# Loading the first halves of k and v as float32 on SyncE's queue and casting them on the chip, with a new order of an attention and SoLU feed-forward kernel

## Chip, cores and metric

The kernel runs on one core of one Trainium2 chip. Its time is device microseconds of one execution; before the change it is 185.19 us, the median of 3 runs (184.95 to 185.66). Lower is better. The profile and the trace are of one execution of 185.46 us.

## What is computed

Linear attention for 8 batches, 8 heads, 576 positions of 64 (first a 64x64 product of k and v for each head, then q times it, then an RMS norm with gain `g_norm`), and behind it a feed-forward layer over 4608 tokens of 512 with 1024 hidden channels, a SoLU activation and a layer norm.

```python
def _attn_ref(q, k, v, g_norm) -> np.ndarray:
    kv = np.einsum('bhsd,bhse->bhde', k, v)
    out = np.einsum('bhsd,bhde->bhse', q, kv)
    rms = np.sqrt(np.mean(out * out, axis=-1, keepdims=True) + 1e-06)
    return (out / rms * g_norm).astype(np.float32)

def _moe_ref(x, w_in, w_out, g_ln) -> np.ndarray:
    h = x @ w_in
    h_max = np.max(h, axis=-1, keepdims=True)
    e = np.exp(h - h_max)
    sm = e / (np.sum(e, axis=-1, keepdims=True) + 1e-09)
    solu = h * sm
    mu = np.mean(solu, axis=-1, keepdims=True)
    var = np.mean((solu - mu) ** 2, axis=-1, keepdims=True)
    ln = (solu - mu) / np.sqrt(var + 1e-06) * g_ln
    return (ln @ w_out).astype(np.float32)
```

## The kernel before

The work is cut into nine token blocks of 512: blocks 0 to 7 are positions of one batch each, block 8 (`q_last`) holds the last positions of all batches. Every step is a named piece: `k.0.1` is the load of k for batch 0, half 1 of the heads (heads 4 to 7; half 0 is heads 0 to 3; from batch 2 on a load has all heads). A text, `ORDER`, lists all pieces by name, with the engine behind a colon where a piece may run on either of two; each engine runs its own pieces in that order. A second text, `ROOMS`, gives the buffer that each tile takes, and `WARM` the number of matmuls in each filler piece `warm.i`. A filler multiplies a tile of zeros (L296) and is read by nothing.

The pieces of one block, with their lines:

- `k`, `v`, `q` (L314), `w_in` (L333), `w_out` (L338): loads issued by POOL, on POOL's queue. k, v, q and w_in are float32 in memory and are cast to bfloat16 by the load. Eight semaphores serve these loads in turn, so the ninth waits until the first has landed. `g_rep` (L324): two loads on SP's queue that bring the 64 values of `g_norm` as a column, one value a partition; they wait for the first load of POOL (L143). `g_rows` (L254): g_ln as 8 rows of 128, on SP's queue.
- `ident` (L280): POOL makes two identity tiles. `turn_g` (L285): PE turns the rows of g_ln; `g_mean` (L287): DVE copies the result and spreads it over a tile for the mean of `w_out`.
- `kv_mm` (L364): PE multiplies k and v; `kv` (L232): three copies of the result a half, on DVE or ACT; `qT_mm` (L404) and `qT` (L232): PE turns q, DVE or ACT copies it out (blocks 4 to 8 are turned by SP's DMA, L412); `o_mm` (L423): q times kv.
- `sq` (L236, ACT), `s_mm` (L435, PE), `ex` (L449 in block 0, L443 later) with `ln` (L439) before it in blocks 1 to 8: the norm's factor; `x` (L455, DVE): o times `g_rep` times the factor. `table` (L460) is ACT's change of function table between block 0 and the rest.
- `h` (L492, PE): x times w_in, 8 column groups of 4 matmuls; in blocks 0 to 2 a group is two pieces, `h.c.f.0` with the first half of `w_in` and of x, `h.c.f.1` with the second. `exp` (L499, ACT), `u` (L503, DVE), `usq` (squares, L236 on ACT or L238 on POOL), `es` (sums of e, L511, POOL), `ua` and `usqa` (folds, L535, DVE), `sums` (L554, PE), `turn`, `stats`, `rstd`: the statistics of the layer norm.
- `w_mean` (L592) and `w_center` (L598): g_ln times `w_out`, less its mean over the channels; `out` (L611, PE): u times that; `ob` (L244 on DVE, L242 on ACT): times the norm's factor; `store` (L627; L623 for block 8).

What sets the order around the change is the head of `ORDER`:

```
v.0.1 k.0.1 q.0.1 ident q.0.0 v.0.0 k.0.0 q.1.0 k.1.0 v.1.0 warm.0 turn_g w_in.0 warm.1 kv_mm.0.1 warm.2 qT_mm.0.1
kv.0.1.1 kv.0.1.0:act qT.0.1:act warm.3 qT_mm.0.0 g_mean kv.0.1.2 o_mm.0.1 sq.0.1.0 warm.4 s_mm.0.1.0 w_in.1 v.1.1
```

Of the kernel before, what the change touches and what calls it, by code (L numbers as in the profile page):

```python
# [20 lines left out]
v.0.1 k.0.1 q.0.1 ident q.0.0 v.0.0 k.0.0 q.1.0 k.1.0 v.1.0 warm.0 turn_g w_in.0 warm.1 kv_mm.0.1 warm.2 qT_mm.0.1  # L21
kv.0.1.1 kv.0.1.0:act qT.0.1:act warm.3 qT_mm.0.0 g_mean kv.0.1.2 o_mm.0.1 sq.0.1.0 warm.4 s_mm.0.1.0 w_in.1 v.1.1
q.1.1 sq.0.1.1 s_mm.0.1.1 qT.0.0 ex.0.1.1 warm.5 kv_mm.0.0 kv.0.0.2:act kv.0.0.0:act kv.0.0.1:act warm.6 o_mm.0.0
ex.0.1.0 g_rep.0 k.1.1 g_rep.1 qT_mm.1.0 w_out.0 qT.1.0 w_out.1 x.0.1.1 x.0.1.0 sq.0.0.0 warm.7 s_mm.0.0.0 sq.0.0.1
warm.8 s_mm.0.0.1 ex.0.0.1 ex.0.0.0 table warm.9 kv_mm.1.0 q.2.0 x.0.0.1 kv.1.0.2 kv.1.0.1 kv.1.0.0 x.0.0.0 warm.10
o_mm.1.0 sq.1.0.0 warm.11 h.0.0.0 sq.1.0.1 v.2.0 k.2.0 s_mm.1.0.0 h.0.4.0 h.0.1.0 ln.1.0.0 h.0.2.0 s_mm.1.0.1 ex.1.0.0
ln.1.0.1 ex.1.0.1 x.1.0.0 h.0.3.0 h.0.0.1 h.0.3.1 h.0.1.1 h.0.4.1 exp.0.3 exp.0.4 q.3.0 u.0.3 h.0.5.0 exp.0.1 h.0.2.1
u.0.4 h.0.5.1 exp.0.2 x.1.0.1 qT_mm.1.1 h.0.7.0 qT.1.1 exp.0.5 exp.0.0 u.0.2 h.0.6.0 h.0.7.1 es.0.1 v.3.0 usq.0.4:act
h.0.6.1 u.0.0 u.0.5 u.0.1 exp.0.7 kv_mm.1.1 h.1.0.0 kv.1.1.2:act kv.1.1.1:act kv.1.1.0:act es.0.0 k.3.0 exp.0.6
o_mm.1.1 w_mean.0 u.0.7 u.0.6 ua.0.0 sq.1.1.1 w_mean.1 sq.1.1.0 s_mm.1.1.1 h.1.4.0 ln.1.1.1 s_mm.1.1.0 w_mean.2  # L30
w_mean.3 ln.1.1.0 ex.1.1.1 ua.0.1 ex.1.1.0 x.1.1.1 v.4.0 w_mean.4 w_mean.5 w_mean.6 w_mean.7 x.1.1.0 h.1.1.0
usq.0.2:act usq.0.3:act usq.0.0:act h.1.1.1 w_center.2 w_center.5 exp.1.1 h.1.0.1 qT_mm.2.0 h.1.2.0 usq.0.7 es.0.2
es.0.3 qT.2.0:act h.1.2.1 h.1.4.1 h.1.6.0 w_center.1 exp.1.2 h.1.6.1 exp.1.0 u.1.1 w_center.0 w_center.4 exp.1.6 u.1.2
usq.0.1 usq.0.6 h.1.7.0 h.1.7.1 exp.1.4 qT_mm.2.1 u.1.0 usq.0.5 exp.1.7 u.1.6 qT.2.1:act w_center.3 out.0.2.0 h.1.5.0
h.1.5.1 q.4.0 kv_mm.2.0 w_center.7 exp.1.5 q.5.0 h.1.3.0 w_center.6 es.1.2 h.1.3.1 kv.2.0.2 kv.2.0.0:act kv.2.1.0:act
kv.2.1.2:act kv.2.1.1:act kv.2.0.1:act out.0.1.0 usq.1.0:act o_mm.2.0 u.1.7 u.1.4 out.0.1.1 out.0.1.2 usq.1.1:act
usqa.0.0 sq.2.0.1 qT_mm.3.1 out.0.1.3 sq.2.0.0 u.1.5 exp.1.3 s_mm.2.0.1 out.0.2.1 s_mm.2.0.0 out.0.2.2 usqa.0.1
ln.2.0.1 u.1.3 usq.1.6:act usq.1.2 sums.0 qT.3.1 ln.2.0.0 out.0.2.3 usq.1.7 usq.1.4 ex.2.0.1 turn.0 o_mm.2.1 stats.0
qT_mm.3.0 sq.2.1.0 x.2.0.1 out.0.3.0 rstd.0 out.0.3.1 qT.3.0 es.1.0 ex.2.0.0 s_mm.2.1.0 out.0.3.2 ob.0.1 ln.2.1.0
out.0.3.3 x.2.0.0 kv_mm.3.0 sq.2.1.1 ob.0.2 ex.2.1.0 s_mm.2.1.1 kv.3.0.1 ln.2.1.1 kv.3.1.2 kv.3.0.2 kv.3.0.0 out.0.0.0  # L40
out.0.0.1 out.0.0.2 es.1.1 k.4.0 x.2.1.0 kv.3.1.1:act kv.3.1.0:act ex.2.1.1 o_mm.3.0 out.0.0.3 sq.3.0.0 x.2.1.1
h.2.0.0 usq.1.3 usq.1.5 sq.3.0.1 s_mm.3.0.0 ob.0.3 o_mm.3.1 ln.3.0.0 h.2.0.1 ob.0.0 store.0.3 sq.3.1.1 s_mm.3.0.1
out.1.1.0 ua.1.0 ln.3.0.1 store.0.1 exp.2.0 ex.3.0.0 usqa.1.0 sq.3.1.0 out.1.1.1 h.2.1.0 h.2.1.1 qT.4 x.3.0.0 es.1.3
h.2.3.0 h.2.3.1 ex.3.0.1 u.2.0 exp.2.1 h.2.5.0 x.3.0.1 exp.2.3 s_mm.3.1.1 es.2.0 h.2.5.1 u.2.1 ln.3.1.1 ex.3.1.1
h.2.7.0 h.2.7.1 u.2.3 ua.1.1 h.2.2.0 s_mm.3.1.0 exp.2.7 qT.5 h.2.2.1 x.3.1.1 usq.2.3 ln.3.1.0 h.2.4.0 u.2.7 h.2.4.1
exp.2.2 h.2.6.0 usqa.1.1 ex.3.1.0 store.0.2 h.2.6.1 u.2.2 exp.2.4 kv_mm.4.0 es.2.1 exp.2.5 es.2.2 usq.2.7 x.3.1.0
store.0.0 sums.1 u.2.4 h.3.4.1 kv.4.0.1:act turn.1 kv.4.1.0:act exp.2.6 kv.4.0.2 kv.4.1.2:act kv.4.1.1:act stats.1
h.3.5.1 kv.4.0.0:act exp.3.4 u.2.5 rstd.1 o_mm.4.1 u.2.6 h.3.2.1 exp.3.5 usq.2.1 ob.1.1 sq.4.1.1 h.3.6.1 u.3.5 exp.3.2
ua.2.0 s_mm.4.1.1 sq.4.1.0 out.1.3.0 exp.3.6 s_mm.4.1.0 u.3.4 ln.4.1.1 k.5.0 out.1.3.1 u.3.2 ln.4.1.0 o_mm.4.0 ob.1.3
ex.4.1.1 h.3.0.1 usq.2.2 v.5.0 sq.4.0.1 u.3.6 h.3.7.1 sq.4.0.0 x.4.1.1 q.6.0 ex.4.1.0 s_mm.4.0.1 s_mm.4.0.0 out.1.2.0  # L50
ln.4.0.1 x.4.1.0 q_last.0 ln.4.0.0 h.3.3.1 ex.4.0.1 h.3.1.1 es.3.2 es.2.3 ex.4.0.0 x.4.0.1 exp.3.3 out.1.2.1 x.4.0.0
usq.2.4:act exp.3.7 es.3.1 h.4.1.1 h.4.6.1 ob.1.2 usq.2.6:act u.3.3 exp.3.1 h.4.0.1 v.6.0 k.6.0 exp.4.6 u.3.1 usq.3.4
exp.3.0 kv_mm.5.0 u.4.6 exp.4.1 h.4.2.1 es.3.3 kv.5.0.1 kv.5.1.1 exp.4.0 kv.5.0.0:act kv.5.1.0 u.3.7 h.4.3.1 u.3.0
usq.2.5 exp.4.2 kv.5.0.2 h.4.7.1 kv.5.1.2:act exp.4.3 usq.2.0:act es.3.0 q.7.0 u.4.1 u.4.0 o_mm.5.1 out.1.0.0
out.1.0.1 u.4.2 sq.5.1.1 u.4.3 sq.5.1.0 usqa.2.0 exp.4.7 s_mm.5.1.1 s_mm.5.1.0 ln.5.1.1 out.2.3.0 ua.2.1 ln.5.1.0
h.4.5.1 ex.5.1.1 usqa.2.1 out.2.3.1 x.5.1.1 usq.3.0 exp.4.5 ob.1.0:act sums.2 usq.3.6:act o_mm.5.0 store.1.0 u.4.5
turn.2 stats.2 out.2.0.0 sq.5.0.1 sq.5.0.0 usq.3.5 u.4.7 out.2.0.1 store.1.1 ex.5.1.0 es.4.3 usq.3.2 s_mm.5.0.0
s_mm.5.0.1 qT.6 x.5.1.0 ln.5.0.0 out.2.1.0 ln.5.0.1 ua.3.0 out.2.1.1 ex.5.0.0 store.1.3 h.4.4.1 ex.5.0.1 x.5.0.0
rstd.2 x.5.0.1 kv_mm.6.0 exp.4.4 usq.4.6 out.2.2.0 kv.6.1.0:act kv.6.0.2 kv.6.0.1:act kv.6.1.2 usq.4.5:act
kv.6.1.1:act ob.2.0 es.4.0 usq.3.1 usq.3.7 h.5.7.1 ob.2.3 usq.3.3:act h.5.6.1 u.4.4 exp.5.7 store.2.3 h.5.3.1 u.5.7  # L60
kv.6.0.0:act usq.4.2:act ua.3.1 exp.5.6 o_mm.6.1 o_mm.6.0 exp.5.3 out.2.2.1 u.5.6 v.7.0 sq.6.0.1 u.5.3 es.4.2
out.3.3.0 ob.2.1 sq.6.0.0 s_mm.6.0.1 out.3.3.1 k.7.0 ob.2.2 sq.6.1.1 out.4.0.0 store.2.2 usqa.3.0 ln.6.0.1 sq.6.1.0
ex.6.0.1 s_mm.6.0.0 store.2.0 ln.6.0.0 out.4.0.1 s_mm.6.1.1 usqa.3.1 x.6.0.1 ex.6.0.0 es.4.1 h.5.2.1 store.1.2
ln.6.1.1 x.6.0.0 h.5.1.1 exp.5.2 qT.7 ex.6.1.1 s_mm.6.1.0 u.5.2 h.5.4.1 usq.4.7 usq.4.1 ln.6.1.0 x.6.1.1 sums.3
exp.5.4 out.3.0.0 turn.3 exp.5.1 es.5.3 stats.3 ex.6.1.0 u.5.4 rstd.3 es.5.1 x.6.1.0 out.3.1.0 h.5.0.1 u.5.1
# [616 lines left out]
```

## Time and profile before

| | |
|---|---|
| median of 3 runs | 185.19 us |
| the profiled execution | 185.46 us |
| its span in the profile | 183.2 us |
| PE busy | 173.1 us, 94% |
| ACT busy | 153.7 us, 84% |
| DVE busy | 142.0 us, 77% |
| POOL busy | 111.7 us, 61% |
| fillers on PE (`warm_ps`) | 44 recorded, 14.3 us |
| moved by DMA | 29.66 MB |

The span is measured from the program's first instruction to its last; the rest of an execution's time lies around it. PE is TensorE's matmuls, PEld its weight loads, DVE VectorE, ACT ScalarE, POOL GpSimd, SP SyncE. Matmuls are pipelined, so PE's busy time is more than the sum of its issue slots. A view lists the releaser behind an arrow: the event that ended the idle time before an instruction. "DMA to landing" is the time from a load's issue to its last byte. GB/s count the bytes as written, so a load that casts float32 to bfloat16 shows half of what it reads.

### The profile page before, as it was taken

How to read it: one execution, taken by the hardware profiler on the slowest of the kernel's cores; microseconds unless marked ns; L12 is line 12 of the kernel's file. 1: busy time of each engine (PE TensorE's matmuls, PEld its weight loads, DVE VectorE, ACT ScalarE, POOL GpSimd, SP SyncE). 2: the span in 40 equal slices, each digit the busy share in tenths (PEclk: the TensorE clock that was granted, in tenths of full speed). 3: DMA queues.
4: the chain of work that ended last, by engine and by line, in shares of the span. 5: the costliest groups of instructions: out<-in, count | busy, mean ns of one | idle time of the engine just before them, and what ended most of it. 6: DMA issues, size and time to landing. Idle time of an engine off the chain costs nothing.

```text
span 183.2 us, 4530 instructions
## 1 busy us (share of the span) xinstructions
PE 173.1 (94%) x1763; PEld 82.1 (45%) x1788; DVE 142.0 (77%) x263; ACT 153.7 (84%) x275; POOL 111.7 (61%) x120
## 2 busy tenths in 40 slices
...
GB/s 52 177 161 209 209 239 396 212 208 210 206 207 184 161 265 51 74 200 190 202 169 216 67 167 265 221 106 96 137 202 27 46 188 58 4 59 111 178 171 173
DMA packets 35030, 29.66 MB, mean 162 GB/s; under 512 B 16441, under 2 KB 28993, under 8 KB 35009
## 3 DMA queue, kind: packets, MB, share of 16 engines
...
q8 instruction: 14, 0.23, 0.5%
...
## 4 chain that ended last, share of the span: by engine, by line
PE 81%; ACT 9%; DVE 7%; issue 2%; ACTq 0%
PE out_ps L611 32%; PE h_ps L492 29%; PE warm_ps L296 6%; PE s_ps L435 4%; PE o_ps L423 3%; PE kv_ps L364 3%; DVE w_out_sb L598 3%; PE sum_ps L554 3%; ACT e_sb L499 3%; ACT osq_sb L236 2%; DVE x_sb L455 2%; ACT kvd L232 1%; DVE u_sb L503 1%; PE qt_ps L404 1%; ACT usq_sb L236 1%
## 5 line engine op out<-in xcount | busy, mean ns | idle before, releaser
L492 PE MATMUL h_ps<-x_sb,w_in_sb 128*128 128x512 bf16 x277 | 67.9, 379 | 1.5 <-DVE x_sb L455 1.0
L611 PE MATMUL out_ps<-w_out_sb,u_sb 128*128 128x512 bf16 x277 | 68.2, 379 | 0.9 <-issue 0.5
L511 POOL TENSOR_TENSOR es_sb<-e_sb 128x512 bf16<-128x512 f32 x36 | 45.6, 1277 | 24.3 <-DVE usq_sb L535 12.4
L503 DVE TENSOR_TENSOR u_sb<-h_ps,e_sb 128x512 bf16<-128x512 f32 x72 | 47.1, 683 | 4.7 <-ACT e_sb L499 4.3
L499 ACT ACTIVATE e_sb<-h_ps,zero_t 128x512 f32<-128x512 f32 x72 | 47.4, 691 | 3.2 <-PE h_ps L492 2.2
L238 POOL TENSOR_TENSOR usq_sb<-u_sb 128x512 bf16<-128x512 bf16 x34 | 34.9, 1041 | 13.0 <-DVE ua_sb L535 7.1
L492 PEld LDWEIGHTS <-w_in_sb 128*128 128x128 bf16 x288 | 27.2, 98 | 33.8 <-issue 3.2
L611 PEld LDWEIGHTS <-u_sb 128*128 128x128 bf16 x288 | 27.1, 98 | 32.2 <-issue 1.6
L455 DVE SCALAR_TENSOR_TENSOR x_sb<-o_ps,g_rep,rst_sb 128x512 bf16<-128x512 f32 x36 | 26.3, 746 | 9.5 <-ACT rst_sb L443 6.4
L236 ACT ACTIVATE usq_sb<-u_sb,zero_t 128x512 bf16<-128x512 bf16 x38 | 26.3, 723 | 0.2 <-DVE u_sb L503 0.2
L236 ACT ACTIVATE osq_sb<-o_ps,zero_t 128x512 bf16<-128x512 f32 x36 | 23.2, 692 | 1.7 <-PE o_ps L423 1.6
L443 ACT ACTIVATE rst_sb<-lss_sb,zero_t 128x512 f32<-128x512 f32 x32 | 22.7, 732 | 0.2
L439 ACT ACTIVATE lss_sb<-s_ps,eps_t 128x512 f32<-128x512 f32 x32 | 21.4, 695 | 0.8 <-PE s_ps L435 0.7
L244 DVE TENSOR_SCALAR ob_sb<-out_ps,rstd 128x512 f32<-128x512 f32 (+1 forms) x25 | 18.0, 735 | 5.1 <-PE out_ps L611 2.5
L535 DVE TENSOR_TENSOR usq_sb<-usq_sb 128x2048 bf16<-128x2048 bf16 (+1 forms) x18 | 17.1, 952 | 0.1
L296 PE MATMUL warm_ps<-zeros 128*128 128x512 bf16 x44 | 14.3, 452 | 1.6 <-DVE zeros L259 1.2
L232 ACT CAST kvd<-kv_ps 64x128 bf16<-64x128 f32 (+1 forms) x26 | 6.6, 263 | 10.2 <-DVE kvd L232 9.5
L232 DVE CAST kvd<-kv_ps 64x128 bf16<-64x128 f32 (+1 forms) x22 | 6.2, 287 | 9.5 <-PE kv_ps L364 8.8
L435 PE MATMUL s_ps<-osq_sb,head_mean 128*128 128x512 bf16 x36 | 13.0, 378 | 0.5 <-ACT osq_sb L236 0.2
L314 POOL DMA_DIRECT2D v_sb<-in_v_dram x10 | 7.7, 775 | 8.1 <-PE mean_ps L592 2.9
L242 ACT ACTIVATE ob_sb<-out_ps,rstd 128x512 f32<-128x512 f32 (+1 forms) x12 | 7.9, 668 | 5.6 <-PE out_ps L611 5.1
L535 DVE TENSOR_TENSOR ua_sb<-u_sb 128x2048 bf16<-128x2048 bf16 x9 | 10.9, 1217 | 0.0
...
## 6 DMA issues: line engine op xcount, KB each, us to landing
out_dram<-ob_sb SPq DMA_DIRECT2D x65, 128.0 KB, 2.4
v_sb<-in_v_dram POOLq DMA_DIRECT2D x6, 576.0 KB, 12.5
...
```

The lines of the kernel that those rows point to most:

```text
L236: nc.scalar.activation(out=dst, in_=src, func=AF.Square, bias=zero_t[:, :])
L238: on[engine].tensor_tensor(out=dst, in0=src, in1=src, op=MUL)
L296: nc.tensor.matmul(t[:, :], zeros[:, 0:128], zeros[:, :], start=True, stop=True)
L439: nc.scalar.activation(out=t[:, :], in_=T["s", i][:, :], func=AF.Ln, bias=eps_t[:, :])
L443: nc.scalar.activation(out=t.rearrange("p a b c -> p (a b c)"), in_=T["lss", i][:, :], func=AF.Exp, scale=-0.5, bias=zero_t[:, :])
L455: nc.vector.scalar_tensor_tensor(out=t[:, 2 * hf:2 * hf + 2, z], in0=T["o", c, hf, z][:, :, :, :], scalar=g_rep[:, :], in1=T["rst", (c, hf ...
L492: nc.tensor.matmul(bank(("h", c, f), [128, 512])[:, :], w_in_sb[:, dt, f * 128:(f + 1) * 128], T["x", c][:, dt].rearrange("p a b c -> p (a ...
L499: nc.scalar.activation(out=t[:, f % 2, :], in_=T["h", c, f][:, :], func=AF.Exp, bias=zero_t[:, :])
L503: nc.vector.tensor_tensor(out=t[:, f, :], in0=T["h", c, f][:, :], in1=T["e", c, f // 2][:, f % 2, :], op=MUL)
L511: on[engine].tensor_tensor(out=t[:, n, :], in0=e[:, 0, :], in1=e[:, 1, :], op=ADD)
L535: nc.vector.tensor_tensor(out=to[:, 0:n, :], in0=src[:, 0:n, :], in1=src[:, n:2 * n, :], op=ADD)
L611: nc.tensor.matmul(bank(("out", c, m), [128, d_model])[:, :], T["u", c][:, f, m * 128:(m + 1) * 128], w_out_sb[:, f, :], start=(f == 0), s ...
```

## The change

Four things are altered.

1. The first two loads, `k.0.1` and `v.0.1`, are split: a piece `wide.v` or `wide.k` loads the half as float32 on SP's queue, into a buffer of the `u` tiles, and the pieces `v.0.1` (DVE) and `k.0.1` (ACT) cast it to bfloat16.
2. `g_norm` is no longer spread by 64-row loads; it is loaded twice into one further row of `g_rows`, turned together with g_ln, and copied with it. `x` takes its column from there and so waits for `g_mean`. The loads of g stand behind the wide loads on SP's queue.
3. `WARM` goes from 12 fillers with 47 matmuls to 6 with 30.
4. `ORDER` and `ROOMS` are new throughout; some copies, squares and scalings change engine. The last two stores are both issued by ACT.

```diff
-14 11 3 3 3 1 2 1 1 3 3 2
+14 5 2 3 4 2
...
-    g_rep = big.tile([128, 1], FP32, name="g_rep")
...
-    nc.sync.dma_start(g_rows[:, :], moe_g_ln.rearrange("(n p) -> n p", p=128))
+    g_sb = big.tile([128, NF + 1], FP32, name="g_sb")
+    g_ln_sb, g_rep = g_sb[:, 0:NF], g_sb[:, NF:NF + 1]
+    g_rows = big.tile([NF + 1, 128], FP32, name="g_rows")
...
+    def load_g(_):
+        for half in range(2):
+            nc.sync.dma_start(g_rows[NF:NF + 1, 64 * half:64 * half + 64], g_norm[None, :])
+        nc.sync.dma_start(g_rows[0:NF, :], moe_g_ln.rearrange("(n p) -> n p", p=128))
...
-    add("turn_g", "pe", turn_g, ["ident"], [("g",)])
+    add("g_rows", "sp", load_g)
+    add("turn_g", "pe", turn_g, ["ident", "g_rows"], [("g",)])
...
+    def load_wide(name, src, hs):
+        t = kept_tile(("u", name), [128, NP // 2, 9 * D], FP32)
+        nc.sync.dma_start(t[:, :, :], rows_of(src, 0, hs, 9))
+
+    def narrow(engine, name, hs):
+        t = kept_tile((name, 0), [128, NP, 9, D], BF16)
+        copy(engine, t.rearrange("p n j d -> p n (j d)")[:, hs.start // 2:hs.stop // 2], T["u", name][:, :, :])
...
-    def load_g(half):
-        nc.sync.dma_start(g_rep[64 * half:64 * half + 64, :], g_norm[:, None])
...
+                if b == 0 and g == 1 and name != "q":
+                    add(("wide", name), "sp", lambda _, a=(name, src, hs): load_wide(*a), [], [("u", name)])
+                    add((name, b, g), "dve|act", lambda e, a=(name, hs): narrow(e, *a), [("wide", name)], [("u", name), (name, b)])
+                    continue
...
-                add(("x", i), "dve", lambda _, i=i: x_mul(*i), [("ex", i), ("g_rep", 0), ("g_rep", 1)], [("o", *i), ("rst", i), ("x", c)])
+                add(("x", i), "dve", lambda _, i=i: x_mul(*i), [("ex", i), "g_mean"], [("o", *i), ("rst", i), ("x", c)])
```

The head of the new `ORDER`:

```
wide.v v.0.1 wide.k k.0.1:act ident g_rows q.0.1 q.0.0 k.0.0 v.0.0 k.1.0 v.1.0 q.1.0 w_in.0 warm.0 qT_mm.0.1 w_in.1
qT.0.1:act kv_mm.0.1 turn_g kv.0.1.1 kv.0.1.2:act qT_mm.0.0 k.1.1 kv.0.1.0:act o_mm.0.1 qT.0.0 sq.0.1.1 sq.0.1.0 v.1.1
```

What this does to the queues is seen at three places. POOL's first work, before (the numbers tell buffers apart; `q_sb_150` comes twice, for half 1 and then half 0 of batch 0):

```order
L314 DMA v_sb_146<-in_v_dram 128x2x576
L314 DMA k_sb_148<-in_k_dram 128x2x576
L314 DMA q_sb_150<-in_q_dram 128x2x512
masks.py:197 MEMSET ident_77 128x128
masks.py:199 ISA
masks.py:199 AFFINE_SELECT ident_77<-ident_77 128x128 [waits Pool_49]
masks.py:197 MEMSET eye_78 8x8
masks.py:199 AFFINE_SELECT eye_78<-eye_78 8x8 [waits Pool_49]
L314 DMA q_sb_150<-in_q_dram 128x2x512
```

And now:

```order
masks.py:197 MEMSET ident_75 128x128
masks.py:199 ISA
masks.py:199 AFFINE_SELECT ident_75<-ident_75 128x128 [waits Pool_49]
masks.py:197 MEMSET eye_76 9x9
masks.py:199 AFFINE_SELECT eye_76<-eye_76 9x9 [waits Pool_49]
L320 DMA q_sb_163<-in_q_dram 128x2x512 x2
L320 DMA k_sb_150<-in_k_dram 128x2x576
L320 DMA v_sb_146<-in_v_dram 128x2x576
L320 DMA k_sb_168<-in_k_dram 128x2x576
```

The five instructions of `ident` stand ahead of the loads instead of behind the third, the two loads of k and v for half 1 are gone, and the loads begin with the two halves of q.

SP's first work, before (`g_rows` and `g_rep` are the loads of g_ln and g_norm, then come the stores of block 0 and the turns of q by DMA):

```order
L254 DMA g_rows<-in_moe_g_ln_dram 8x128
L324 DMA g_rep<-in_g_norm_dram 64x1 [waits DMASW0_49]
L324 DMA g_rep<-in_g_norm_dram 64x1
L627 DMA out_dram<-ob_sb 64x512 [waits DVE_49]
L627 DMA out_dram<-ob_sb 64x512 x3
```

And now:

```order
L326 DMA u_sb<-in_v_dram 128x2x576
L326 DMA u_sb<-in_k_dram 128x2x576
L279 DMA g_rows<-in_g_norm_dram 1x64 x2
L280 DMA g_rows<-in_moe_g_ln_dram 8x128
L639 DMA out_dram<-ob_sb 64x512 [waits DVE_49]
```

The two wide loads come first, without a wait; the loads of g follow them.

ACT's first work, before (`kvd` are the copies of the kv products, `osq` the squares of `sq`, `rst` the results of `ex`):

```order
L246 ACT_TABLE_LOAD
L232 CAST kvd_1_0_101<-kv_ps 128x128 [waits DVE_49]
L232 COPY qT_sb<-qt_ps 128x1024 [waits PE_49]
L236 ACTIVATE osq_sb<-o_ps,zero_t 128x512 [waits PE_49] x2
L449 ACTIVATE rst_sb<-s_ps,eps_t 128x512 [waits PE_49]
L232 CAST kvd_0_2_100<-kv_ps 64x128 [waits PE_49]
```

And now:

```order
L244 ACT_TABLE_LOAD
L230 CAST k_sb<-u_sb 128x1152 [waits DMAHW1_49]
L230 COPY qT_sb<-qt_ps 128x1024 [waits PE_49]
L230 CAST kvd_1_2_101<-kv_ps 64x128 [waits DVE_49]
L230 CAST kvd_1_0_99<-kv_ps 128x128
L234 ACTIVATE osq_sb<-o_ps,zero_t 128x512 [waits PE_49]
```

The cast of k stands ahead of everything else on ACT and waits for SP's second load (`DMAHW1`); the copy of q, the kv copies and the squares are queued behind it. On DVE the cast of v stands at the same place and waits for the first.

168 lines of the change are left out of this document (81 added, 87 removed).

## The prediction

> **What bounds the kernel now.** I read the stages first (busy time by stretch), then the chain of work that ended last, then the loads. The first rows are the profile page's span and its chain by engine; below them is the view by stretches (start:end in us, length, then busy us and instructions of PE, PE's weight loads, DVE, ACT and POOL, the granted clock, the DMA engines' busy share, GB/s).
>
> ```profile
> span 183.2 us, 4530 instructions
> PE 81%; ACT 9%; DVE 7%; issue 2%; ACTq 0%
> ```
> ```profile
> 0.00:7.00 7.00, 5.80 (x15) 2.02 (x15) 0.78 (x12) 1.28 (x1) 5.81 (x15) 1.00 0.65 94
> ...
> 16.00:22.20 6.20, 5.33 (x71) 2.40 (x72) 4.28 (x8) 5.17 (x9) 2.98 (x4) 1.00 1.15 211
> ...
> 26.00:38.00 12.00, 10.35 (x92) 5.48 (x93) 10.76 (x16) 11.81 (x23) 6.36 (x8) 1.00 1.24 294
> 38.00:50.00 12.00, 11.18 (x161) 5.93 (x162) 11.28 (x19) 11.03 (x21) 9.10 (x10) 1.00 1.22 208
> 50.00:66.00 16.00, 15.73 (x189) 7.40 (x181) 15.56 (x30) 15.88 (x30) 10.46 (x10) 1.00 1.16 195
> ...
> 140.00:179.40 39.40, 38.92 (x325) 18.09 (x328) 31.63 (x58) 30.52 (x54) 17.52 (x15) 1.00 0.42 102
> ```
>
> From 50 us on PE hardly rests (15.73 of 16, 38.92 of 39.4). What is saved before that moment is saved at the end; what is saved on another engine after it is not. Between 26 and 50 us ACT is the fullest (11.81 of 12, then 11.03) and DVE close behind. Before 22 us PE looks busy, but much of that is filler. The chain in order of time (start, us, what) says what was waited for:
>
> ```profile
> 1.20 5.80 PE warm_ps L296 x14
> ...
> 7.15 2.48 PE warm_ps L296 x11
> 9.63 0.69 PE kv_ps L364 x36
> ...
> 12.62 0.46 PE o_ps L423 x8
> ...
> 14.98 0.70 PE kv_ps L364 x36
> ...
> 15.71 0.26 ACT kvd L232
> ...
> 18.19 0.75 DVE x_sb L455
> ...
> 22.43 0.43 PE h_ps L492 x2
> ...
> 49.75 0.63 PE sum_ps L554 x32
> ...
> 179.43 0.48 ACT ob_sb L242
> ```
>
> The first 25 fillers end at 9.63, and then comes `kv_mm.0.1`. The second product, `kv_mm.0.0`, starts at 14.98, the first `h` at 22.43. So the kernel is a start of some 22 us, an ACT-bound stretch to about 50, and a PE-bound rest. Behind the last matmul lie 3.8 us to the span's end. The change acts on the start. What holds it up, with one group of instructions a line (start, us; in brackets idle time and releaser):
>
> ```profile
> 14.91 0.65 PEld L364 LDWEIGHTS <-k_sb 64*64 64x64 bf16 x36 [0.42 <-DMA k_sb<-in_k_dram]
> ...
> 20.33 1.28 ACT L460 ACT_TABLE_LOAD   x1
> ...
> 21.94 1.27 ACT L236 ACTIVATE osq_sb<-o_ps,zero_t 128x512 bf16<-128x512 f32 x2 [0.33 <-PE o_ps L423]
> ```
>
> `kv_mm.0.0` waits for a load, `k.0.0`. Issue and landing of single loads (issue time ahead of the dash, then us to landing):
>
> ```profile
> L314 POOL DMA_DIRECT2D v_sb<-in_v_dram x1: 890/890/890, 1.3 to 1.3; - x1
> DMA to landing us min/median/max: 4.3/4.3/4.3
> ```
> ```profile
> L314 POOL DMA_DIRECT2D k_sb<-in_k_dram x1: 733/733/733, 5.8 to 5.8; - x1
> DMA to landing us min/median/max: 8.6/8.6/8.6
> ```
> ```profile
> L333 POOL DMA_DIRECT2D w_in_sb<-in_moe_w_in_dram x2: 763/767/771, 8.7 to 9.4; - x2
> DMA to landing us min/median/max: 12.4/13.3/14.2
> ```
>
> `v.0.1` lands at 1.3 + 4.3 = 5.6, `k.0.0`, the sixth half load, at 5.8 + 8.6 = 14.4, the halves of `w_in` at 8.7 + 12.4 = 21.1 and 9.4 + 14.2 = 23.6. The loads run in a row: the start is bound by the bytes.
>
> **Term 1: the loads start earlier.** The same bytes are read before `w_in`, in nearly the same order. How fast, and when:
>
> ```profile
> 3.00:6.50 3.50, 3.50 (x10) 1.24 (x9) 0.00 (x0) 0.00 (x0) 3.35 (x8) 1.00 1.11 170
> ...
> 10.50:12.50 2.00, 2.00 (x21) 1.35 (x20) 1.29 (x4) 1.21 (x2) 0.73 (x1) 1.00 0.89 123
> ...
> 23.60:31.00 7.40, 7.35 (x73) 3.82 (x73) 4.93 (x8) 7.10 (x12) 3.75 (x5) 1.00 1.24 324
> ```
> ```profile
> 59.00:62.00 3.00, 3.00 (x16) 1.35 (x14) 3.00 (x4) 3.00 (x7) 0.81 (x1) 1.00 0.94 218
> ```
> ```profile
> out_dram<-ob_sb SPq DMA_DIRECT2D x65, 128.0 KB, 2.4
> ```
> ```profile
> 0.75 0.41 SPq L254 DMA_DIRECT2D g_rows<-in_moe_g_ln_dram  x1
> ```
> ```profile
> 3.56 0.23 POOL masks.py:197 MEMSET ident<- 128x128 bf16 x1
> ...
> 4.41 0.71 POOL L314 DMA_DIRECT2D q_sb<-in_q_dram  x1
> ```
>
> A half of k or v is 0.295 MB as bfloat16: 1.7 us at 170 GB/s. As float32 it is 0.59 MB: 1.8 us at the 324 GB/s that the uncast `w_out` reaches. The bytes cost the same; the clock of the first one moves. POOL issues its first load at 1.3; SP issues at 0.75. `v.0.1` needed 4.3 us, 1.7 of them bytes, so 2.6 of latency. On SP's queue a 128 KB store lands 2.4 us after issue (page, median), 0.4 of it bytes, so 2.0. Bounds: 0.5 us earlier (same latency) to 1.1 (store's latency); I take 0.9, nearer the row of SP's own queue. POOL's five `ident` instructions now stand ahead of its loads and delay `q.0.1` by 4.41 - 3.56 = 0.85, hidden under 3.6 us of SP's two loads. If these did not run, it would cost 0.85.
>
> **Term 2: the scattered g_norm goes.** Between 10.5 and 12.5 us the rate falls to 123 GB/s. That is when the two loads of `g_rep` are served, 64 rows of 4 bytes each:
>
> ```profile
> L324 SPq DMA_DIRECT2D g_rep<-in_g_norm_dram x2: 582/584/587, 5.6 to 6.2; - x2
> DMA to landing us min/median/max: 7.3/7.3/7.3
> ```
>
> Against 170 GB/s the two us lost 2.0 x 47 / 170 = 0.55 us of loading. Two rows of 256 bytes take their place; if the dip has another cause, the term is 0. I take 0.55.
>
> **Term 3: two queues at once.** SP's float32 and POOL's cast loads overlap for some 4 us. No row shows that. The nearest with both queues is 59:62 (stores beside loads), share 0.94 against 1.20 or so: up to 22% slower, 0.9 us; from below nothing, as one queue alone already fills the engines. I take 0, nearer the many stretches at 1.11 to 1.24, and keep 0.9 in the range. The Trainium skill ("DMA: Bandwidth & Descriptors", section "Queues, rings and completion order") says that each DMA engine goes round its queues packet by packet. By that rule the second SP load would share and land up to 1.8 later, near 8.6; the 7.3 us of `g_rep` are waiting of that kind, and the sum below holds with either value. So `k.0.0` and `v.0.0` are there at 14.4 - 0.9 - 0.55 = 13.0 (12.2 to 14.4), `w_in.0` at 19.6, `w_in.1` at 22.1.
>
> **Term 4: the two casts and the first half.**
>
> ```profile
> 11.55 1.01 ACT L232 COPY qT_sb<-qt_ps 128x1024 bf16<-128x1024 bf16 x1 [0.60 <-PE qt_ps L404]
> 10.88 0.69 DVE L289 TENSOR_SCALAR g_mean<-g_ln_sb 128x1024 fp32r<-128x1024 f32 x1
> ```
>
> 1152 elements cost, scaled by width, 1.1 us on ACT (k) and 0.8 on DVE (v). DVE and ACT are empty then. Wide k lands at 6.8 (alone) to 8.6 (shared); with the cast `kv_mm.0.1` starts at 8.0 to 9.8, against 9.6. Behind k's cast ACT holds the copy of `qT.0.1` (1.0), so `o_mm.0.1` at 9.6 to 11.4, squares (1.27), `s_mm`: PE is free for `kv_mm.0.0` at 11.6 to 13.4. That is beside the 13.0 of the load, so the first half costs 0 or, shared, 0.4. With g_norm turned with g, `x` now waits for `g_mean` on DVE, which stands at about 15, before the first `x`: 0.
>
> **Term 5: from kv_mm.0.0 to ACT's long run.** `kv_mm.0.0` at 13.15 to 13.85; then ACT in its new order: two kv copies (0.55), wait for `o_mm.0.0` (0.45), two squares (1.3), two `ex` (1.3), two kv copies (0.55), one `ex` (0.65), the table (1.3): 19.95. Then `sq.1.0`, which stood at 21.94: 2.0 us gained. The last `x` before `h` ends at 19.4, `w_in.0` lands at 19.6; `h` starts then. The fillers that go (47 to 30) stood in waits; they cost nothing now and give nothing.
>
> **Term 6: the rest of the order.** I counted the pieces on ACT between the table and the sums of token block 0: before 6 `sq`, 5 `ln`, 4 `ex`, 16 `exp`, 7 `usq`, 8 kv and 2 qT copies; now 8, 8, 6, 16, 3, 7 and 2. Seven pieces more, four `usq` and a kv copy fewer: at some 0.65 each (two squares take 1.27; kv 0.26) ACT's work grows by 1.75 us. But five pieces of PE that stood behind those sums now stand ahead of them: one `o_mm`, two `s_mm`, one `qT_mm` and two matmuls of `out`, together about 1.65 us (0.46 from the chain, 0.22 a matmul, 0.45). An end set by ACT up to the sums and PE after it moves by 1.75 - 1.65 = +0.1. Bounds by the rows: PE stands still for 24 - 10.35 - 11.18 = 2.5 us between 26 and 50; a better order could win 1, a worse one lose 2 more. The tail has the same four steps: 0.
>
> **Sum.** -2.0 + 0.1 = -1.9 on the profiled execution's 185.46 us (span 183.2 and 2.26 around it): 183.55. The median of the runs is 185.19, 0.27 lower: **183.3 us**.
>
> **Rivals.**
> 1. *SP's loads are starved by POOL's queue.* For it: `g_rep`'s 7.3 us for 256 bytes. Against it: SP's two loads are queued first. Price: wide k at about 10, `kv_mm.0.1` at 11.2, PE free for `kv_mm.0.0` at 14.6 instead of 14.9: gain 0.3 + 0.1, time 184.9.
> 2. *PE slows down (ends slower).* The chain shows 14 fillers at 0.41 us and the next 11 at 0.225: the array is slow until it has been busy some 5 us. With 16 fillers instead of 33 after the first 14 it could fall back between 7 and 19 us. Price: the start's products at double time (0.7 twice, and about 0.8 of o, qT and s) and 14 of `h` again at 0.19 more, 2.65: in all 4.9, less what waits hide (1.0): 183.3 + 3.9 = 187.2. It decides if the slow state returns before `h`; if only the start is hit and `h` not, the gain is just halved. Against it: the row of 44 to 46 us below, where PE is busy 1.31 of 2.00 and matmuls stay at full speed. In the Trainium skill ("TensorE: Matmul & The Clock Gate", section "Why this matters for your kernels") PE-idle gaps over about 3 us bring the half clock. By that rule the gap of 1 to 2 us behind the fillers does not.
> 3. *The new order stalls later.* Loads issued by POOL behind its squares (`v.3`) or ACT's seven extra pieces make PE wait. For it: ACT at 11.81 of 12. Price 1 to 3 us: 185.3.
> 4. *It doesn't do what it says:* loading is bound by bytes, not by the first one's clock, and the dip was not `g_rep`: 185.2.
>
> ```profile
> 44.00:46.00 2.00, 1.31 (x6) 0.59 (x6) 1.94 (x4) 1.10 (x6) 1.68 (x2) 1.00 1.21 213
> ```
>
> **Chances.** Forecast (182 to 184.2) 0.50, with a better order (below 182) 0.08; rival 1 0.09 and rival 4 0.05, both within 0.5%; rival 2 0.12 (0.10 of it slower); rival 3 0.16 (0.02 faster, 0.07 same, 0.07 slower). A measurement of this kernel can tell 0.5%, 0.9 us: faster means under 184.3, slower over 186.1. Faster 0.60, same 0.23, slower 0.17. The range 181.5 to 186.6 leaves out rival 2 and the best orders.
>
> **What would show it.** In the profile after: `k.0.0` landed near 13 and not 14.4; `kv_mm.0.1` between 8 and 10; the first `h` near 19.7; ACT's second table load ending near 20; the GB/s from 3 to 13 us without a dip to 123; fillers and early products at 0.22 us, not 0.41; the sums of block 0 near 48. I am wrong if `h` starts after 21, or if it starts early and PE stands still for more than 4 us between `h` and the sums.

## The result, and the profile after

The changed kernel takes 182.49 us, the median of 6 runs (182.00 to 183.04), against 185.29 us (184.95 to 185.86) for the kernel before on the same chip: a ratio of 0.9846, with a 95% interval of 0.9819 to 0.9873. It is faster by 2.8 us; 183.3 was forecast. The profiled execution took 182.66 us with a span of 180.5 us, against 185.46 and 183.2. One slow execution each of old_g_24 and fill_none, over 1.5% above the fastest of its kernel, is left out of the times below.

The page's span and its chain of work by engine, after the change:

```profile
span 180.5 us, 4509 instructions
...
PE 66%; DMA 21%; ACT 7%; DVE 3%; issue 1%; POOL 0%; POOLq 0%; ACTq 0%
```

DMA, which had no share of the chain before, now has 21%, PE 66% instead of 81%. Up to 40 us the chain is followed through loads. The same stretches as before the change (length, then PE, weight loads, DVE, ACT, POOL, the granted clock, DMA share, GB/s):

```profile
0.00:7.00 7.00, 5.36 (x14) 1.83 (x14) 1.67 (x13) 1.74 (x2) 6.31 (x16) 1.00 0.72 201
16.00:22.20 6.20, 5.69 (x71) 2.88 (x71) 2.86 (x5) 6.08 (x11) 1.88 (x4) 1.00 1.14 209
26.00:38.00 12.00, 11.16 (x102) 5.87 (x101) 11.63 (x18) 11.47 (x22) 10.07 (x10) 1.00 1.26 272
38.00:50.00 12.00, 11.36 (x246) 6.10 (x243) 11.47 (x21) 11.53 (x21) 8.03 (x10) 1.00 1.16 195
50.00:66.00 16.00, 16.00 (x194) 7.45 (x185) 15.48 (x32) 15.30 (x29) 11.36 (x11) 1.00 1.12 191
```

ACT is fuller from 16 to 22 us (6.08 of 6.2, before 5.17), and PE stands still for 1.5 us between 26 and 50 (24 - 11.16 - 11.36) where it stood still for 2.5. The steps of the start, in the timeline (start, length in us):

```profile
8.11 0.62 PE L416 MATMUL qt_ps<-ident,q_sb 128*128 128x128 bf16 x8 [1.56 <-DMA q_sb<-in_q_dram]
8.66 0.76 PE L376 MATMUL kv_ps<-v_sb,k_sb 64*64 64x64 bf16 x36
...
12.69 0.76 PE L376 MATMUL kv_ps<-v_sb,k_sb 64*64 64x64 bf16 x36
...
18.57 1.28 ACT L472 ACT_TABLE_LOAD   x1
...
19.78 1.03 PE L504 MATMUL h_ps<-x_sb,w_in_sb 128*128 128x512 bf16 x4
...
19.86 0.69 ACT L234 ACTIVATE osq_sb<-o_ps,zero_t 128x512 bf16<-128x512 f32 x1
...
40.60 0.78 PE L376 MATMUL kv_ps<-v_sb,k_sb 64*64 64x64 bf16 x72 [0.44 <-DMA k_sb<-in_k_dram]
...
48.74 0.30 PE L566 MATMUL sum_ps<-ua_sb,stat_sel 128*32 128x128 bf16 x8
```

`kv_mm.0.0` starts at 12.69 (before 14.98), `h` at 19.78 (22.43), `sq.1.0` at 19.86 (21.94), the sums of block 0 at 48.74 (49.75). The loads behind that (issue time ahead of the dash, then us to landing): wide k, `q.0.1`, `k.0.0`, `v.0.0` and the halves of `w_in`.

```profile
L326 SPq DMA_DIRECT2D u_sb<-in_k_dram x1: 454/454/454, 1.3 to 1.3; - x1
...
DMA to landing us min/median/max: 5.3/5.3/5.3
...
L320 POOL DMA_DIRECT2D q_sb<-in_q_dram x1: 882/882/882, 1.6 to 1.6; - x1
...
DMA to landing us min/median/max: 6.4/6.4/6.4
...
L320 POOL DMA_DIRECT2D k_sb<-in_k_dram x1: 716/716/716, 3.2 to 3.2; - x1
...
DMA to landing us min/median/max: 7.7/7.7/7.7
...
L320 POOL DMA_DIRECT2D v_sb<-in_v_dram x1: 721/721/721, 3.9 to 3.9; - x1
...
DMA to landing us min/median/max: 8.4/8.4/8.4
...
L342 POOL DMA_DIRECT2D w_in_sb<-in_moe_w_in_dram x2: 718/726/733, 6.8 to 8.4; - x2
...
DMA to landing us min/median/max: 12.5/13.0/13.5
```

They land at 6.6, 8.0, 10.9, 12.3, 19.3 and 21.9 us. Wide k is there at 6.6, yet PE's first product is the turn of q, and it waits for `q.0.1`. The dip is gone: between 10.5 and 12.5 us the engines move 207 GB/s instead of 123.

```profile
10.50:12.50 2.00, 1.81 (x15) 0.63 (x11) 0.42 (x1) 1.27 (x2) 0.74 (x2) 1.00 1.22 207
```

### The profile page after: what moved, and what is told of

Its sections match the earlier page's. It is cut to its first block, busy times and chain, and to the rows that moved or that the text cites. A ratio compares the mean times of both kernels' runs of the same rounds, so it can differ in the third digit from the quotient of the medians.

```text
span 180.5 us, 4509 instructions
## 1 busy us (share of the span) xinstructions
PE 171.3 (95%) x1771; PEld 80.5 (45%) x1771; DVE 143.4 (79%) x262; ACT 153.8 (85%) x276; POOL 112.1 (62%) x120
## 4 chain that ended last, share of the span: by engine, by line
PE 66%; DMA 21%; ACT 7%; DVE 3%; issue 1%; POOL 0%; POOLq 0%; ACTq 0%
PE out_ps L623 31%; PE h_ps L504 24%; DMA k_sb<-in_k_dram 10%; DMA w_in_sb<-in_moe_w_in_dram 7%; DMA q_sb<-in_q_dram 4%; PE s_ps L447 3%; PE sum_ps L566 2%; PE kv_ps L376 2%; ACT osq_sb L234 2%; PE o_ps L435 2%; DVE u_sb L515 1%; ACT e_sb L511 1%; ACT kvd L230 1%; ACT rst_sb L455 1%; DVE usq_sb L547 1%
## 5 line engine op out<-in xcount | busy, mean ns | idle before, releaser
L511 ACT ACTIVATE e_sb<-h_ps,zero_t 128x512 f32<-128x512 f32 x72 | 46.1, 696 | 2.2 <-PE h_ps L504 2.1
L236 POOL TENSOR_TENSOR usq_sb<-u_sb 128x512 bf16<-128x512 bf16 x36 | 37.0, 1042 | 13.8 <-DVE ua_sb L547 13.6
L467 DVE SCALAR_TENSOR_TENSOR x_sb<-o_ps,g_sb,rst_sb 128x512 bf16<-128x512 f32 x36 | 26.3, 746 | 9.2 <-ACT rst_sb L455 7.5
L234 ACT ACTIVATE usq_sb<-u_sb,zero_t 128x512 bf16<-128x512 bf16 x36 | 24.3, 720 | 1.7 <-DVE u_sb L515 1.7
L242 DVE TENSOR_SCALAR ob_sb<-out_ps,rstd 128x512 f32<-128x512 f32 (+1 forms) x27 | 19.3, 735 | 6.9 <-PE out_ps L623 3.4
L447 PE MATMUL s_ps<-osq_sb,head_mean 128*128 128x512 bf16 x36 | 13.5, 379 | 0.9 <-ACT osq_sb L234 0.6
L320 POOL DMA_DIRECT2D v_sb<-in_v_dram x9 | 6.9, 767 | 6.6 <-PE qt_ps L416 3.8
L298 PE MATMUL warm_ps<-zeros 128*128 128x512 bf16 x30 | 9.7, 468 | 1.2 <-DVE zeros L256 1.2
L230 DVE CAST kvd<-kv_ps 64x128 bf16<-64x128 f32 (+1 forms) x18 | 5.2, 288 | 6.8 <-PE kv_ps L376 6.1
L240 ACT ACTIVATE ob_sb<-out_ps,rstd 128x512 f32<-128x512 f32 (+1 forms) x10 | 6.6, 661 | 4.2 <-PE out_ps L623 4.2
L320 POOL DMA_DIRECT2D q_sb<-in_q_dram x10 | 7.6, 765 | 4.1 <-DVE ua_sb L547 2.1
```

The source lines that it names most:

```text
L234: nc.scalar.activation(out=dst, in_=src, func=AF.Square, bias=zero_t[:, :])
L236: on[engine].tensor_tensor(out=dst, in0=src, in1=src, op=MUL)
L242: nc.vector.tensor_scalar_mul(out=dst, in0=src, scalar1=by)
L467: nc.vector.scalar_tensor_tensor(out=t[:, 2 * hf:2 * hf + 2, z], in0=T["o", c, hf, z][:, :, :, :], scalar=g_rep, in1=T["rst", (c, hf, z)][ ...
L511: nc.scalar.activation(out=t[:, f % 2, :], in_=T["h", c, f][:, :], func=AF.Exp, bias=zero_t[:, :])
```

## The experiments

In each group the kernels ran on one chip beside the kernel before, and every ratio is against that. The changed kernel's is 0.9846. It ran on another chip than the groups below; differences to its 182.49 us are by medians, and the medians of the kernel before agree within 0.2 us (185.29 to 185.47).

**Undoing one load at a time: no_wide and old_g.** The first loads k and v of half 1 through POOL again:

```diff
-wide.v v.0.1 wide.k k.0.1:act ident g_rows q.0.1 q.0.0
+v.0.1 k.0.1 ident g_rows q.0.1 q.0.0
...
-                if b == 0 and g == 1 and name != "q":
+                if False:
```

> The changed kernel with one part undone: the first halves of k and v are loaded by POOL, cast on the way, ahead of ident and q.0.1; there is no float32 load and no cast on chip; order, g_norm and fillers as changed. Theory (the first load starts earlier on SP's queue and so all later ones): k.0.0 and v.0.0 land 0.9 to 1.3 us later than the 10.96 and 12.35 of the changed kernel, v.0.0 at 13.3 to 13.7, the first h at 20.7 to 21.1 instead of 19.78, and the run is 0.9 to 1.3 us longer than the changed one: about 183.5, 0.990 of the kernel before. Rival (the gain is g_norm's dip and the new order alone): h within 0.3 of 19.78, time 182.5, 0.985.

It took 184.15 us, 0.9933 (0.9907 to 0.9959): 1.7 us over the changed kernel, more than the loads were to cost. `v.0.0` landed at 13.3 and `w_in.0` at 20.6, `h` started at 21.07, all as the theory has it (1.0 to 1.3 us later). Some of the rest is in the clock. PE's timeline, from one of the faster executions (183.32 us):

```profile
8.27 0.88 PE L416 MATMUL qt_ps<-ident,q_sb 128*128 128x128 bf16 x8 [1.98 <-DMA q_sb<-in_q_dram]
9.07 1.17 PE L376 MATMUL kv_ps<-v_sb,k_sb 64*64 64x64 bf16 x36
```

and the stretch from 8.5 to 11.5 us, the third number from the right being the granted clock:

```profile
8.50:11.50 3.00, 2.90 (x52) 2.36 (x49) 0.29 (x1) 1.53 (x3) 2.37 (x4) 0.50 1.17 187
```

PE rested for 1.98 us, then had half its clock for 3 us: 36 small matmuls took 1.17 us instead of 0.76. The mean granted clock of every execution is on record, and such a spell takes it from 1.00 to about 0.99 (1.5 of 181 us): of the ten executions of no_wide one had 1.00 and was the fastest (183.16 us), eight had 0.986 to 0.991, and one, with 0.98, was the slowest (185.38). The rival (no gain from the wide loads) falls by `h`'s start. fill_few (below) ran beside no_wide and took 182.42 us, so the changed kernel's level holds on this chip too.

The second brings `g_norm` as 128 rows of 4 bytes again, now behind the two wide loads:

```diff
-            nc.sync.dma_start(g_rows[NF:NF + 1, 64 * half:64 * half + 64], g_norm[None, :])
+            nc.sync.dma_start(g_col[64 * half:64 * half + 64, :], g_norm[:, None])
...
-            out=t[:, 2 * hf:2 * hf + 2, z], in0=T["o", c, hf, z][:, :, :, :], scalar=g_rep,
+            out=t[:, 2 * hf:2 * hf + 2, z], in0=T["o", c, hf, z][:, :, :, :], scalar=g_col[:, :],
```

> The changed kernel with one part undone: g_norm comes again as 64 rows of 4 bytes, two loads on SP's queue behind the two float32 loads; all else as changed. Theory (each such load costs loading time, 0.55 us for the two): q.0.1 to w_in.1 land 0.4 to 0.6 us later, h at 20.2 to 20.4, time 182.9 to 183.1, 0.987 to 0.988. Rival (the dip was waiting of SP's queue behind POOL's and not a cost of the scattered rows): landings within 0.15 of the changed kernel's, time 182.5, 0.985.

185.02 us, 0.9979 (0.9960 to 0.9999): almost the whole gain is lost to 512 bytes, and both expectations were far too low. The loading rate between 5.5 and 9 us, old_g and then the changed kernel:

```profile
5.50:9.00 3.50, 1.72 (x5) 0.39 (x3) 0.54 (x1) 1.15 (x1) 2.12 (x3) 1.00 0.81 124
```
```profile
5.50:9.00 3.50, 1.94 (x33) 1.07 (x33) 0.46 (x1) 1.38 (x2) 2.69 (x4) 1.00 1.14 188
```

3.5 x (188 - 124) / 188 = 1.2 us of loading are lost, and `w_in.0` lands 1.3 us later, at 20.6. Here too the clock adds to it, behind a rest of 2.57 us:

```profile
9.79 0.62 PE L417 MATMUL qt_ps<-ident,q_sb 128*128 128x128 bf16 x8 [2.57 <-DMA q_sb<-in_q_dram]
10.34 1.17 PE L377 MATMUL kv_ps<-v_sb,k_sb 64*64 64x64 bf16 x36
```

**Taking the clock out of it: no_wide_18 and old_g_24.** More fillers ahead of the first product, to bridge the rest:

```diff
-14 5 2 3 4 2
+18 5 2 3 4 2     (no_wide_18)
+24 5 2 3 4 2     (old_g_24)
```

> The kernel no_wide with 18 fillers instead of 14 ahead of the first product, so that PE rests less than 1 us before q.0.1 has landed. Theory (no_wide lost time in two ways: its loads land 0.96 to 1.30 us later, and PE's granted clock falls to 0.50 for 3 us after a rest of 2 us): the clock stays at 1.00 from 8 to 12 us, kv_mm.0.1 takes 0.76 again and not 1.17, loads land as in no_wide (w_in.0 at 20.6), time 0.9 to 1.2 us over the changed kernel's: 183.4 to 183.7, 0.990 to 0.992. Rival (the later loads alone cost it, the clock is hidden in waits): 184.1, 0.9933 as no_wide.

183.93 us, 0.9933 (0.9910 to 0.9956). The four more fillers did not bridge the rest: all 18 ended at 6.5 us, since PE came to full speed sooner in the traced execution, so the rest was 2.12 us all the same and the half clock came back, only later, from about 10.7 to 14 us. But four of the six executions had a mean clock of 0.997 or more, so no such spell. Over both kernels, the five executions without a spell took 183.16 to 184.44 us (median 183.74), the ten with 0.986 to 0.991 took 183.32 to 184.91 (median 184.17). By that the later loads cost some 1.25 us and a spell about 0.4; the two groups overlap, so the second figure is uncertain.

> The kernel old_g (g_norm as 128 rows of 4 bytes) with 24 fillers instead of 14 ahead of the first product, so that PE rests less than 1 us before q.0.1 has landed at 9.75 us. Theory (two losses, as in no_wide: loads 1.2 to 1.6 us later, and PE's clock at 0.50 for 3 us): clock 1.00 throughout, w_in.0 at 20.6, h at 20.9 to 21.1, time 183.5 to 183.9, 0.990 to 0.993. Rival (the later loads alone): 185.0, 0.998.

183.69 us, 0.9926 (0.9903 to 0.9950), as the theory has it. In the trace PE rested for 0.69 us, the clock stayed at 1.00, and `kv_mm.0.1` took 0.76:

```profile
10.13 0.62 PE L417 MATMUL qt_ps<-ident,q_sb 128*128 128x128 bf16 x8 [0.69 <-DMA q_sb<-in_q_dram]
10.68 0.76 PE L377 MATMUL kv_ps<-v_sb,k_sb 64*64 64x64 bf16 x36
```

So of old_g's 2.5 us the scattered rows cost 1.2 by later loads (183.69 - 182.49), and 1.3 by the half clock that comes with their delay (185.02 - 183.69); by the ratios, which set off the chips, it is 1.5 and 1.0. The single executions bear the clock out. Four of old_g_24's five had a mean clock of 0.996 or more and took 183.53 to 183.79 us, the fifth, with 0.989, took 184.71. In old_g all twelve had less than 1: seven with 0.987 to 0.991 have a median of 184.83, five with 0.979 or 0.980, as of two spells, 185.50.

A long rest doesn't always bring the spell. pe_extra (below) has the start of the changed kernel, rested for 2.09 us in its traced execution, longer than no_wide, and kept its clock. PE's row and a stretch:

```profile
7.98 0.62 PE L416 MATMUL qt_ps<-ident,q_sb 128*128 128x128 bf16 x8 [2.09 <-DMA q_sb<-in_q_dram]
```
```profile
7.00:12.00 5.00, 3.68 (x66) 2.32 (x67) 0.98 (x2) 3.68 (x6) 2.39 (x4) 1.00 1.20 198
```

**Fillers: fill_few and fill_none.**

```diff
-14 5 2 3 4 2
+14 1 1 1 1 1     (fill_few)
+1 1 1 1 1 1      (fill_none)
```

> The changed kernel with 19 fillers (14 1 1 1 1 1) instead of 30 (14 5 2 3 4 2). Theory (fillers behind the first 14 stand in waits and neither cost nor help as long as PE stays at full speed): matmuls at 0.22 us through the start, time 182.5, 0.985. Rival (PE falls to its slow state with fewer fillers): products and h at 0.41 us a matmul for a while after 10 us, h about 0.7 to 1.5 later, up to 3.9 in all: 183.2 to 186.4, 0.989 to 1.006.

182.42 us, 0.9842 (0.9819 to 0.9865): no difference. PE now rested for 1.37 us in the middle of the start and stayed fast:

```profile
12.14 0.59 PE L447 MATMUL s_ps<-osq_sb,head_mean 128*128 128x512 bf16 x2 [1.37 <-ACT osq_sb L234]
```

> The changed kernel with 6 fillers (1 at each of the six places) instead of 30, so that PE hardly works before 8 us. Theory: PE is in its slow state from 8 us until it has been busy some 4 us; the first products, o, qT and s take double time (0.7 twice, some 0.8 and some more), h starts 1.0 to 2.5 us later and its first dozen matmuls may still be slow: 183.5 to 186.4, 0.990 to 1.006. Rival (the slow state is hidden in the waits for loads): h within 0.5 of 19.78, time 182.5 to 183.0, 0.985 to 0.988.

184.25 us, 0.9939 (0.9909 to 0.9969): 1.8 us over the changed kernel, in the theory's window; `h` came 2.8 us later in the traced execution (185.49 us), more than it allowed. Without the first 14 fillers PE is slow from its first product to the first `h`, and its first four matmuls still take 1.16 us together instead of 1.03:

```profile
8.83 1.17 PE L376 MATMUL kv_ps<-v_sb,k_sb 64*64 64x64 bf16 x36
...
22.59 1.16 PE L504 MATMUL h_ps<-x_sb,w_in_sb 128*128 128x512 bf16 x4 [0.34 <-DVE x_sb L467]
```

The granted clock reads 1.00 through all of this. The half speed that PE starts at isn't seen in that column here, only in the matmuls' own lengths; the one that comes back after a rest (no_wide, old_g) is seen in both.

**Parts of the change on the old order: b_rows and b_wide_rows.** The first is the kernel before with only the rows of `g_norm`; the second has the wide loads and fewer fillers as well. Everything else runs in the order of before.

```diff
-v.0.1 k.0.1 q.0.1 ident q.0.0
+v.0.1 k.0.1 q.0.1 ident g_rows q.0.0                        (b_rows)
+wide.v v.0.1 wide.k k.0.1:act q.0.1 ident g_rows q.0.0      (b_wide_rows)
...
```

> The kernel before with one part of the change: g_norm as two rows of 256 bytes, issued on SP's queue at the start and turned with g; no float32 loads, order and fillers as before. Theory (each of the 128 rows of 4 bytes takes engine time wherever it is served): no dip at 10.5 to 12.5 us, k.0.0 lands 0.5 to 1.5 us before 14.45, w_in.0 as much before 21.10, first h at 21.0 to 21.9 instead of 22.4, time 184.0 to 184.9, 0.992 to 0.997. Rival (it cost so much only in old_g, where q.0.1 stood behind it): landings within 0.2, time 185.4, 1.000.

184.54 us, 0.9950 (0.9931 to 0.9969). `k.0.0` landed at 13.5 (before 14.4), `w_in.0` at 20.6 (21.1), and `h` started at 21.67. The rate from 9.5 to 12.5 us, before and in b_rows, and what the engines were doing in that time before (queue, packets, MB, share of 16 engines; q1 is SP's queue):

```profile
9.50:12.50 3.00, 2.84 (x58) 2.13 (x58) 1.43 (x4) 1.21 (x2) 1.37 (x2) 1.00 1.00 145
```
```profile
9.50:12.50 3.00, 2.84 (x45) 1.93 (x40) 1.89 (x5) 1.30 (x3) 1.47 (x3) 1.00 1.20 199
```
```profile
q0 software_dynamic: 403, 0.43, 95.1%
q1 hardware_dynamic: 151, 0.00, 5.3%
```

SP's 151 packets took 5.3% of the engines by their own time, but a quarter of the rate. Their price doesn't stand in their own duration; it is read from what the other queue lost. The theory holds, the rival falls.

> The kernel before with the float32 loads, the rows of g_norm and fewer fillers (14 3 3 3 1 1 1 1 1 1 2 2), but the order of before for all else. Theory (most of the gain is the earlier start of h, and before's order gets at least half of it): k.0.0 at about 12.3, h at 20.3 to 21.3 since before's order has more on ACT ahead of it, time 183.4 to 184.4, 0.989 to 0.995; what is left to 182.5 is the new order's. Rival (the parts need the new order to pay): h at 21.5 or later, time 184.8 or more, 0.997 and over.

184.29 us, 0.9935 (0.9913 to 0.9958). Time, `h` and `k.0.0` fall into the theory's windows, but the old order gets 0.65% of the 1.54%, not quite the half. The interval overlaps that of b_rows: on the old order the wide loads bring nothing that can be told (0.25 us by the medians), though `w_in.0` landed 1.65 us earlier than there, at 19.0. PE's timeline, from the slowest of the six executions (185.08 us):

```profile
13.62 0.76 PE L380 MATMUL kv_ps<-v_sb,k_sb 64*64 64x64 bf16 x36
...
18.35 0.75 PE L380 MATMUL kv_ps<-v_sb,k_sb 64*64 64x64 bf16 x36 [0.28 <-DVE x_sb L471]
...
20.98 0.59 PE L508 MATMUL h_ps<-x_sb,w_in_sb 128*128 128x512 bf16 x2
...
83.00 0.77 PE L380 MATMUL kv_ps<-v_sb,k_sb 64*64 64x64 bf16 x72 [0.78 <-DVE u_sb L519]
```

`k.0.0` was there at 12.0, but `kv_mm.0.0` started at 13.62, and `h` at 20.98, 2 us after its load. Here the chain of pieces is late, not the loads: it lets 0.69 us through to `h` (21.67 in b_rows). As much is still there at the sums of block 0 (48.45 against 49.14) and of block 1 (66.37, 67.06). Behind them it is lost, in this execution by the wait of 0.78 us at 83 us, which b_rows doesn't have, and by 0.6 us from the last sums to the last `ob` (7.05 us, in b_rows 6.46). b_wide_rows also has other buffers (`ROOMS`) than b_rows; whether these bring the waits, and whether the faster executions have them too, no run here shows.

The new order, with its fillers and its choice of engines, is worth 1.8 us on top (184.29 - 182.49, the intervals apart). `h` starts 1.2 us earlier with it (19.78). The sums of block 0 come as late (48.74), but with the new order some 1.65 us of PE's work that stood behind them is done by then. The new order without the other parts was not run.

**What binds between `h` and the sums: act_extra, pe_extra, load_extra.**

```diff
-        nc.scalar.activation(out=t[:, f % 2, :], in_=T["h", c, f][:, :], ...)
+        for _ in range(2 if c == 0 and f in (1, 5) else 1):
+            nc.scalar.activation(out=t[:, f % 2, :], in_=T["h", c, f][:, :], ...)
```

> The changed kernel with exp.0.1 and exp.0.5 executed twice each, so that ACT has 1.3 us more to do between 24 and 31 us and nothing else is touched. Theory A (the stretch from h to the sums of block 0 is ACT's, as the prediction has it): the sums and the end 1.0 to 1.3 us later, 183.5 to 183.8, 0.990 to 0.992. Theory P (PE's, from the first h on): 0 to 0.3 us, 182.5 to 182.8. Theory L (the loads' up to k.2 at 40.56 us): 0 to 0.4 us, 182.5 to 182.9, 0.985 to 0.987.

183.67 us, 0.9899 (0.9871 to 0.9928): 1.2 us later for 1.3 us of work, as theory A has it. The sums of block 0 start at 49.86 us (48.74), 0.28 of it lost ahead of `h` already.

```diff
+        extra = (-1, -1) if c == 0 and dts[0] == 0 and f in (2, 3, 5) else ()
-        for dt in dts:
+        for dt in (*extra, *dts):
+            d = max(dt, 0)
...
```

> The changed kernel with six more matmuls of 0.216 us in h.0.2, h.0.3 and h.0.5 (each first matmul three times), so that PE has 1.3 us more to do between 25 and 31 us. Theory A (ACT's stretch): 0 to 0.3 us, 182.5 to 182.8. Theory P (PE's): 1.1 to 1.3 us, 183.6 to 183.8, 0.991 to 0.992. Theory L (the loads': PE waits 0.50 us for w_out and 0.44 us for k.2, and these waits take up the additional matmuls): 0.2 to 0.5 us, 182.7 to 183.0, 0.986 to 0.988.

183.62 us, 0.9903 (0.9869 to 0.9938): 1.1 us later, as theory P has it, and against theory A; the sums start at 49.99. Both intervals just reach the changed kernel's (up to 0.9873), but the sums move with the medians. So neither engine alone binds. ACT's rows in pe_extra show how PE's work gets onto ACT's path (the execution traced, 185.02 us, is the slowest of the seven, and PE waits 1.34 us more in it at 70 us, behind the sums):

```profile
26.21 1.84 ACT L513 ACTIVATE e_sb<-h_ps,zero_t 128x512 f32<-128x512 f32 x3 [0.57 <-PE h_ps L506]
28.37 0.69 ACT L513 ACTIVATE e_sb<-h_ps,zero_t 128x512 f32<-128x512 f32 x1 [0.31 <-PE h_ps L506]
...
31.25 1.27 ACT L234 ACTIVATE osq_sb<-o_ps,zero_t 128x512 bf16<-128x512 f32 x2 [0.53 <-PE o_ps L435]
```

ACT waits for later `h` and `o_mm`; the chain goes from one engine to the other several times, and work on either lengthens it. PE's wait for `k.2` (0.44 us) is gone in both kernels and the end came later all the same: theory L, by which that load decides, falls, although the chain of work gives `k.2`'s load 10% of the span. The chain names what came last at one moment, by 0.44 us; it does not say how close the next one is.

```diff
-        nc.gpsimd.dma_start(...)
+        for _ in range(2 if (name, b) == ("v", 2) else 1):
+            nc.gpsimd.dma_start(...)
```

> The changed kernel with v.2 loaded twice, so that 1.4 us more of loading stands ahead of k.2. k.2 lands at about 41.9 to 42.4 us instead of 40.56 and kv_mm.2.0 starts then. Theory L (the loads decide up to k.2): end 1.1 to 1.8 us later, 183.6 to 184.3, 0.991 to 0.995. Theory A (ACT's stretch, k.2's landing is beside it): 0 to 0.5 us, 182.5 to 183.0, 0.985 to 0.988. Theory P lies between: PE's wait of 0.44 us becomes 1.8, of which some comes back, 183.0 to 183.8.

194.32 us, 1.049 (1.0456 to 1.0524). This is none of the three theories, because the second load of `v.2` writes the same tile and so waited on POOL until the first had landed. POOL's row, PE's, and a stretch:

```profile
38.14 0.74 POOL L321 DMA_DIRECT2D v_sb<-in_v_dram  x1 [17.39 <-DMA v_sb<-in_v_dram]
```
```profile
43.15 1.01 PE L417 MATMUL qt_ps<-ident,q_sb 128*128 128x128 bf16 x8 [5.15 <-DVE u_sb L516]
```
```profile
42.00:50.00 8.00, 2.32 (x12) 1.28 (x12) 2.69 (x4) 3.16 (x6) 7.97 (x9) 0.50 1.22 207
```

POOL's sums of e stood behind that wait for 17.39 us, ACT's `exp` waited for POOL, DVE's `u` for `exp`, PE for `u`, and PE's clock fell to 0.50 for some 13 us (41 to 54). For the loads it is inconclusive; it prices a wait on POOL that looks like a mere load.

**A change of the first half: qT_dve.**

```diff
-qT.0.1:act kv_mm.0.1 turn_g kv.0.1.1
+qT.0.1 kv_mm.0.1 turn_g kv.0.1.1
```

> The changed kernel with two moves in the start: POOL issues q.0.1 ahead of ident, and DVE instead of ACT copies qT.0.1 (0.7 us beside ACT's two kv copies). On the queues: if POOL's first load waits until SP's float32 loads are through, q.0.1 lands at 8.0 as before; if the queues share, 0.3 us or more earlier. On the first half: o_mm.0.1 at 9.9 to 10.1 instead of 10.38, kv_mm.0.0 at 12.35 to 12.45 (v.0.0's landing) instead of 12.69, h at 19.4 to 19.6 (w_in.0's landing) instead of 19.78. Theory (the first half's chain and the loads are about level): 0.1 to 0.4 us faster, 182.1 to 182.4, 0.983 to 0.985. Rival (moves of the first half are lost in the waits for loads): 182.5, 0.985.

The kernel that ran holds only the second of the two moves: `ident` still stands ahead of `q.0.1`. (b_wide_rows has the other order: `q.0.1`, issued at 1.25 us instead of 1.63, landed at 7.85 instead of 8.03.) 181.81 us, 0.9823 (0.9787 to 0.9858): the best median, but its interval holds the changed kernel's. In its trace `o_mm.0.1` starts at 10.27 (10.38), `kv_mm.0.0` at 12.58 (12.69) and `h` at 19.66 (19.78): 0.1 us that can be followed, less than the theory's windows for all three. The two kv copies on ACT waited for DVE's, which now stands behind the turned q.

## Why the prediction was right, step by step

The time lies 0.8 us under the forecast, inside the range and in its likeliest case. Forecast for the profiled execution was -1.9 us; it moved by -2.8. The path of the start was right; in terms 1 and 6 the sizes were off, and in term 5 two misses cancel.

- **Term 1, loads earlier (-0.9).** Right in kind, too small. The wide loads bring `w_in.0` 1.3 us (no_wide) to 1.65 us (b_wide_rows against b_rows) earlier, over the bound of 1.1 taken from latencies alone. `k.0.0`, forecast for 13.0 together with `v.0.0`, landed at 10.9, since it is now loaded ahead of `v.0.0`, which landed at 12.3.
- **Term 2, the dip (-0.55).** Right: b_rows lands `k.0.0` 0.95 and `w_in.0` 0.5 us earlier. Behind wide loads (old_g) 128 such rows cost 1.2.
- **Term 3, two queues (0).** Right in the sum, for another reason. Wide k landed at 6.6, as if alone, not near 8.6. (By the rule weighed there, of the Trainium skill, "DMA: Bandwidth & Descriptors", section "Queues, rings and completion order", the queues would have shared; the trace shows no sharing, but not whether POOL's load had work ready for the engines by then.) It was POOL that paid: from 1 to 4.5 us only SP's queue moved anything, 357 packets, and `q.0.1`, issued at 1.6, took 6.4 us where `v.0.1` in no_wide, the first load on POOL's queue there, took 4.2.

```profile
q1 hardware_dynamic: 357, 0.79, 66.6%
```

- **Term 4, first half.** All three windows held: `kv_mm.0.1` at 8.66 (8.0 to 9.8), `o_mm.0.1` at 10.38 (9.6 to 11.4), `kv_mm.0.0` at 12.69 (11.6 to 13.4). But what PE's first product waits for is `q.0.1`, not k's cast. Little of that is `ident`'s doing: issued 0.38 us earlier, ahead of `ident`, `q.0.1` landed 0.2 earlier (b_wide_rows).
- **Term 5 (-2.0).** Right in the sum, with some luck: the table ends at 19.85 (19.95 forecast), `sq.1.0` moved by 2.08, `h` starts at 19.78 (19.6 to 19.7). But `kv_mm.0.0` started 0.46 us earlier than the 13.15 that the sum begins with, and ACT's pieces behind it took 0.36 longer. ACT's first copies had to wait for a copy on DVE, a wait that the sum left out:

```profile
13.81 0.54 ACT L230 CAST kvd<-kv_ps 64x128 bf16<-64x128 f32 x2 [0.33 <-DVE kvd L230]
```

- **Term 6 (+0.1): the term that was mis-sized.** It measured -0.6. From `sq.1.0` to the sums, before and after (fourth engine: ACT):

```profile
21.94:49.75 27.81, 25.34 (x247) 12.95 (x249) 22.68 (x35) 26.51 (x48) 16.86 (x19) 1.00 1.22 245
```
```profile
19.86:48.74 28.88, 27.40 (x269) 13.60 (x267) 24.38 (x38) 27.98 (x50) 19.66 (x20) 1.00 1.24 242
```

  ACT's work grew by 1.47 (26.51 to 27.98; 1.75 was forecast), but its idle time fell from 1.30 to 0.90, so the stretch grew by only 1.07. Less the 1.65 us of PE's work that no longer stands behind the sums, that is -0.58. That count was right: from the sums to the last `ob` it is 128.55 us (48.74 to 177.29), before 130.19 (49.75 to 179.94). With -2.08 it makes -2.66 of the -2.80; most of what is left, 0.1, lies outside the span (2.16 us around it instead of 2.26). That the stretch is ACT's was half the truth: act_extra and pe_extra show a chain through both.
- **Rival 1** (SP starved): its mirror image happened, see term 3. **Rival 2** (slow PE) didn't happen here, with a rest of 1.56 us and a clock at 1.00, but it is real and close by: behind rests of 1.98 and 2.57 us PE had half its clock for about 3 us, which cost 1.0 to 1.3 us of time in old_g. The Trainium skill ("TensorE: Matmul & The Clock Gate", section "Why this matters for your kernels") puts the limit near 3 us; these rests were shorter, and the measurement decides. The length of the rest isn't the whole condition, since pe_extra's 2.09 us left the clock alone. The fillers behind the first 14 don't decide it (fill_few is as fast); the spells come with the wait for `q.0.1` behind the first 14. Where only the start is slow the rival had the gain halved; fill_none, slow to the first four matmuls of `h`, loses 1.8 of 2.8 us. **Rival 3** (worse order): the opposite, put on last the order brings 1.8 us. The parts don't add up, though: put into the old order the rows bring 0.9 us (185.47 - 184.54) and the wide loads 0.25, taken out of the changed kernel they cost 2.5 and 1.7. Part of that is the half clock; in the traces of the old order PE rests for no more than 0.6 us at a time between its first filler and `h`. **Rival 4** falls by no_wide, old_g and b_rows.
